# Second MLP: a plain tile of 256 tokens, four tiles of 512 by half-block products, and a plain last group

## The chip, the cores and the metric

The kernel runs on one core of a Trainium2 chip. The metric is the device time of one execution in microseconds (us); a lower one is better. Three executions of the kernel before took 1023.52, 1023.8 and 1024.66 us, median 1023.8.

## The reference

Three stages follow one another, all in fp32: causal attention with a bias for 4 sequences of 576 tokens and 8 heads of 64, a first MLP with softplus, a second MLP with a rational function. The change touches the second MLP:

```
x = _moe_ref(x=x, ...)                  # [2304, 512], the first MLP
h = x @ w_in                            # [2304, 512] @ [512, 2048]
P = a[0] + a[1]*h + a[2]*h*h + a[3]*h*h*h
Q = 1.0 + |b[0]|*|h| + |b[1]|*h*h
g = P / (Q + 1e-06)
return g @ w_out                        # [2304, 2048] @ [2048, 512]
```

## The kernel before

Every product of matrices is made of three products of fp32r parts: high by high, high by low, low by high. An operand therefore comes as a pair (`gh` and `gl` for g, `xh` and `xl` for x, `wh` and `wl` for a weight): ScalarE copies the high part, and GpSimd or VectorE subtracts it to get the low one.

The 2048 hidden units are 16 blocks of 128 (`ff`). For a tile of tokens and a block, the *first product* makes h in a bank of PSUM (tiles `h` and `at`, two banks each), an elementwise chain makes g, and the *second product* adds g times w_out to the output banks (`acc`, four of them, 128 tokens by 512 each).

The elementwise chain of a block is: ScalarE makes a = |h| (L1201, L1238), t (L1203, L1240) and w (L1202, L1239); GpSimd multiplies w by a (L1204, L1241); VectorE multiplies t by h and adds (L1205 and L1206, L1242 and L1243); then `quotient`: ScalarE Ln (L1219) and Exp (L1220), VectorE three passes (L1221 to L1223); then ScalarE copies the high part (L1395, L1254) and GpSimd makes the low one (L1397, L1255). The exponential is written back into the block's bank of PSUM, so that the bank comes free only after the last VectorE pass, L1223. In the first five blocks of the first tile (`H_ONLY`) it goes to SBUF instead.

The tiles of the second MLP are listed in `T2`: one *plain* tile of 384 tokens, three of 512, one plain tile of 384 (`TAIL`). In a plain tile the first product of a block is 12 products of all the tile's tokens (L1092 to L1094), the second is 3 for each 128 tokens (L1135 to L1137).

In a tile of 512 the blocks go in four groups (`q`), each of two by two half-blocks: a pair of hidden blocks i, and two halves j of the tokens. Four half-block pairs of first products are made of seven *slots* (`SLOTS`, L1340) in place of eight, from sums and differences of weights and of tokens; a slot is 12 products of 256 columns. The sums of slots are taken through a save in SBUF (ScalarE, L1361) and an addition (VectorE, L1366). `out_part` (L1269 to L1271) makes the second products. The operands of the slots are split by ScalarE and GpSimd (L1291, L1292), the weight parts `wa` come from DRAM by DMA.

While the first plain tile runs, VectorE, ScalarE and GpSimd still convert weights of the second MLP (L907 to L914), and the first three blocks are interleaved with the end of the first MLP.

The order of instructions on each engine is fixed by a planner (`plan`), which follows costs of operations up to the planned time `UNTIL`; what comes later stays in the order in which the events were written. Every engine takes its instructions in that order.

The last tile is copied out of PSUM by ScalarE and VectorE in turn (`evacuate`); the last 128 tokens go in two halves (L1156 to L1159).

Of the kernel before, what the change touches and what calls it, by code (L numbers as in the profile page):

```python
# [17 lines left out]
T2 = [(0, 384)] + [(384 + t * 512, 512) for t in range(3)] + [(1920, 384)]  # L18
TAIL = 4
# [4 lines left out]
KD = DM // 128  # L24
NF = DFF // 128
NEG = -8.0e9
LAST = (1, TAIL, 15)
# [41 lines left out]
UNTIL = 936.0  # L69
# [269 lines left out]
def moe_chain_kernel(ctx, tc, qk0, v0, qk, vv, s0, s, w1, w2, ab, out):  # L339
# [703 lines left out]
    def split_x_(ph, T, k):  # L1043
        n = TILES[ph][T][1]
        if n <= 256:
            t = t_xs([128, 2, 256])[:, :, 0:n]
            hi, lo = t[:, 0], t[:, 1]
        elif ph == 1 and k == 0:
            hi, lo = (y_t[T][:, KD + i] for i in range(2))
        elif (ph, T) == (1, TAIL):  # L1050
            hi, lo = (t_l("xl", [128, 512], F32R)[:, 0:n] for _ in range(2))
        else:
            hi, lo = t_xs([128, 512])[:, 0:n], t_xs([128, 512])[:, 0:n]
        if ph == 0:
            for b, s0, w, o in segments(T):
                nc.scalar.activation(hi[:, o:o + w], x_t[b][:, k, s0:s0 + w], AF.Copy)
                nc.vector.tensor_tensor(lo[:, o:o + w], x_t[b][:, k, s0:s0 + w], f(hi[:, o:o + w]), op=ALU.subtract)
        else:
            src = f(y_t[T][:, k])
# [6 lines left out]
    def load_y(T):  # L1066
        plain = T in (0, TAIL)
        y_t[T] = t_x("yt", [128, KD + 2 * plain, T2[T][1]], F32R if plain else F32)
        for a, o, n in pieces(*T2[T]):
            dst = y_t[T][:, 0:KD, o:o + n]  # L1070
            nc.sync.dma_start(out=f(dst) if plain else dst, in_=y_d[a])
# [5 lines left out]
    def stage_a_(u):  # L1077
# [6 lines left out]
        else:  # L1084
            wh, wl = w2_t[ff, 0] if T == 0 else (None, None)
        for k in range(KD):
            xh, xl = xs_t[ph, T, k]
            cs = slice(k * 128, (k + 1) * 128)
            if (ph, T) == (1, TAIL):
                w, cs = wa_t[T, ff // 4, f"a{ff % 2 + 1}{k // 2 + 1}"][:, ff // 2 % 2], slice(k % 2 * 128, k % 2 * 128 + 128)  # L1090
                wh, wl = w[:, 0], w[:, 1]
# [49 lines left out]
    def evacuate(ph, T, acc):  # L1141
# [10 lines left out]
        for m, a in enumerate(acc):  # L1152
            if (ph, T, m) == (1, TAIL, 2):
                ya, yb = (tmp_tile("PA", 3, (128, 256)) for _ in range(2))
                o = out[t0 + 256:t0 + 384, :]
                nc.scalar.activation(ya, a[:, 0:256], AF.Copy)  # L1156
                nc.vector.tensor_copy(yb, a[:, 256:512])
                nc.sync.dma_start(out=o[:, 0:256], in_=ya)
                nc.scalar.dma_start(out=o[:, 256:512], in_=yb)  # L1159
                return  # L1160
# [23 lines left out]
    def stage1_(u):  # L1184
# [11 lines left out]
        else:  # L1196
# [7 lines left out]
            (nc.vector if u == LAST else nc.gpsimd).tensor_tensor(w, w, a, op=ALU.mult)  # L1204
# [4 lines left out]
    def stage2(u):  # L1209
# [4 lines left out]
        r, o = (h_t[u],) * 2 if T or ff >= H_ONLY else (a, w)  # L1214
# [10 lines left out]
    class Block:  # L1225
        def __init__(self, T, q, i, j):
            self.T, self.q, self.i, self.j = T, q, i, j
            self.ends = q == 3 and i != j

    w_no = [0]  # L1230

    def act1(bl):
        h = bl.h
        a = tmp_tile("e", 2)
        t = tmp_tile("PA", 3, (128, 512))
        w = tmp_tile(*(("P4", 2), ("tc", 3), ("tmp", 1), ("tc", 3))[w_no[0] % 4], (128, 512))
        w_no[0] += 1
# [6 lines left out]
        bl.g = (t, w, a)  # L1244

    def act2(bl):
        t, w, a = bl.g
        quotient(a, t, w, bl.h, bl.h)
        bl.g = t

    def act3(bl):
        gh = tmp_tile("gh", 3, dt=F32R)
        gl = tmp_tile("gl", 3, dt=F32R)
        nc.scalar.activation(gh, bl.g, AF.Copy)  # L1254
        nc.gpsimd.tensor_tensor(gl, bl.g, f(gh), op=ALU.subtract)  # L1255
        bl.g = (gh, gl)
# [3 lines left out]
    def out_part(bl, p):  # L1260
        gh, gl = bl.g
# [17 lines left out]

    ops_t = {}  # L1280

    def operand_steps(T):
# [6 lines left out]
        def split(name, src):  # L1289
            hi, lo = ops_t[T, name] = new(name), new(name)  # L1290
# [3 lines left out]
        def minus(o, x, z):  # L1294
# [95 lines left out]
    def stage3_(u):  # L1390
# [5 lines left out]
        eng = nc.vector if in_bank(u) or u == LAST else nc.gpsimd  # L1396
# [4 lines left out]
    if True:  # L1401
# [195 lines left out]
        for T in range(1, TAIL):  # L1597
            at = 28 * (T - 1)
            for q in range(4):
                group(T, q, at + 7 * q, events)  # L1600
            events.append((at + 9.3, lambda T=T: load_y(T + 1)))
            for n in range(7):
                events.append(((at - 5.7 + n if T > 1 else 0.01 + 0.05 * n if n < 2 else 0.5 + 0.9 * n), lambda T=T, n=n: operand(T, n)))
        at = 28 * (TAIL - 1) + 1

        def tail_a(u):
            stage_a(u)
            used[0] += u[2] % 4 == 3 and 4
            load_wa(used[0] + WA_AHEAD)

        for k in range(KD):
            events.append((at - 4 + k, lambda k=k: split_x(1, TAIL, k)))
        for ff in range(NF):
            u = (1, TAIL, ff)
            for t, fn in ((0, tail_a), (0.1, stage1), (1.5, stage2), (2.9, stage3), (4.3, stage_b)):
                events.append((at + 1.4 * ff + t, lambda u=u, fn=fn: fn(u)))
# [65 lines left out]
```

## Time and profile before

| | |
|---|---|
| median of three executions | 1023.8 us |
| profiled execution, its own time | 1024.89 us |
| span of the profiled execution | 1023.1 us |
| granted TensorE clock, mean | 1.000 |
| busy: TensorE | 998.2 us (98%) |
| busy: ScalarE | 803.2 us (79%) |
| busy: VectorE | 791.1 us (77%) |
| busy: GpSimd | 466.4 us (46%) |

The span reaches from the first to the last instruction; the execution's own time is 1.8 us longer. The first plain tile of the second MLP runs from about 616 to 687 us, the three half-block tiles follow to 940, the last plain tile to 1019. In the tables, PE is TensorE's products, PEld its weight loads, DVE VectorE, ACT ScalarE, POOL GpSimd; SPq and ACTq are the queues from which transfers are issued. Busy times of products overlap, so what one product costs is read from start to start.

### The profile page before, as it was taken

Reading aid. Unit: us, or ns where it says so; the run is one execution under the profiler, and the core shown is the slowest. Engines: PE = TensorE matmul, PEld = TensorE weight load, DVE = VectorE, ACT = ScalarE, POOL = GpSimd, SP = SyncE. Lnnn points to the kernel's source line nnn. Section 1 sums busy time; section 2 is a strip of 40 time slices with the busy share of each in tenths; the row PEclk is TensorE's granted clock in tenths of the full one; section 3 lists DMA queues with packets and bytes.
Section 4 is the critical chain, followed back from the end, with each engine's and each line's share of the span. In section 5 each row is a group of like instructions: output and inputs, shape, how many; then the busy total and the mean of one; then the engine's idle time right before and its main releaser. Section 6 shows DMA issues by size and latency. Waiting matters only on the chain. (4 is left out here: it accounts for less than half of the span.)

```text
span 1023.1 us, 18253 instructions
## 1 busy us (share of the span) xinstructions
PE 998.2 (98%) x5924; PEld 903.1 (88%) x5924; DVE 791.1 (77%) x1783; ACT 803.2 (79%) x1652; POOL 466.4 (46%) x464
## 2 busy tenths in 40 slices
PE   6999999999999999999999999999999999999998
PEld 5889999898999888988999999888888998889897
DVE  5888987878897888786677549888788778777765
ACT  5898878887887777777767778888779878788775
POOL 2756665311220121121445666765567457555542
PEclk9999999999999999999999999999999999999999
DMA  9877566565554653435999998528456656555300
GB/s 249 292 253 240 189 220 215 167 206 163 154 189 145 194 166 121 121 101 173 370 342 336 300 351 285 184 83 273 168 167 208 206 168 191 206 169 160 124 1 31
DMA packets 101071, 201.63 MB, mean 197 GB/s; under 512 B 11249, under 2 KB 30513, under 8 KB 100977
## 3 DMA queue, kind: packets, MB, share of 16 engines
q1 hardware_dynamic: 98432, 196.31, 58.6%
q10 hardware_dynamic: 2544, 4.16, 1.6%
q8 instruction: 47, 0.77, 0.3%
q14 instruction: 48, 0.39, 0.1%
HBM read 161.16 MB, written 35.19 MB: 192 GB/s over the span
## 5 line engine op out<-in xcount | busy, mean ns | idle before, releaser
L614 POOL TENSOR_SCALAR PA<-PA,stat 128x384 f32<-128x384 f32 (+3 forms) x112 | 70.8, 638 | 173.1 <-DVE stat L613 65.7
L1092 PE MATMUL h<-xs,w1h 128*128 128x448 f32 (+1 forms) x360 | 122.8, 342 | 1.6 <-DVE e L1194 1.5
L1093 PE MATMUL h<-xs,w1h 128*128 128x448 f32 (+1 forms) x360 | 122.7, 341 | 0.0
L1094 PE MATMUL h<-xs,w1l 128*128 128x448 f32 (+1 forms) x360 | 122.1, 340 | 0.0
L1129 PE MATMUL acc<-gl,w1h 128*128 128x448 f32 (+1 forms) x352 | 118.9, 339 | 1.2 <-POOL gl L1397 1.2
L1130 PE MATMUL acc<-gh,w1l 128*128 128x448 f32 (+1 forms) x352 | 118.5, 340 | 0.8 <-DMA w1l<-l_d 0.7
L1128 PE MATMUL acc<-gh,w1h 128*128 128x448 f32 (+1 forms) x352 | 118.6, 340 | 0.0
L1255 POOL TENSOR_TENSOR gl<-PA,gh 128x512 fp32r<-128x512 f32 x48 | 63.2, 1319 | 69.8 <-issue 55.9
L611 ACT ACTIVATE PA<-PA,stat 128x384 f32<-128x384 f32 (+3 forms) x112 | 64.0, 572 | 17.4 <-DVE stat L594 16.2
L1269 PE MATMUL acc<-w2b,gh 128*128 128x512 f32 x192 | 75.9, 395 | 0.0
L1270 PE MATMUL acc<-w2b,gh 128*128 128x512 f32 x192 | 75.8, 395 | 0.0
L1271 PE MATMUL acc<-w2b,gl 128*128 128x512 f32 x192 | 73.7, 395 | 0.0
L1092 PEld LDWEIGHTS h<-xs,w1h 128*128 128x128 f32 x360 | 67.8, 189 | 5.8 <-DVE e L1194 2.4
L1093 PEld LDWEIGHTS h<-xs,w1h 128*128 128x128 f32 x360 | 67.8, 188 | 3.4
L1094 PEld LDWEIGHTS h<-xs,w1l 128*128 128x128 f32 x360 | 67.8, 189 | 3.1
L1129 PEld LDWEIGHTS acc<-gl,w1h 128*128 128x128 f32 x352 | 66.1, 188 | 4.5 <-POOL gl L1397 1.4
L1130 PEld LDWEIGHTS acc<-gh,w1l 128*128 128x128 f32 x352 | 66.0, 189 | 4.4 <-DMA w1l<-l_d 0.9
L1128 PEld LDWEIGHTS acc<-gh,w1h 128*128 128x128 f32 x352 | 66.1, 189 | 3.0
L1190 ACT ACTIVATE e<-h 128x448 f32<-128x448 f32 (+1 forms) x90 | 43.3, 482 | 30.3 <-PE h L1094 28.6
L1397 POOL TENSOR_TENSOR gl<-e,gh 128x256 fp32r<-128x256 f32 (+1 forms) x48 | 47.4, 989 | 31.1 <-ACT gh L1395 25.6
L594 DVE CUSTOM_DVE_ANT_0 PA<-at,mask 128x384 f32<-128x384 f32 (+3 forms) x100 | 50.5, 518 | 5.7 <-PE at L622 4.2
L621 PE MATMUL at<-ht 128*128 128x512 f32 (+3 forms) x156 | 53.5, 347 | 1.1 <-DVE stat L602 0.8
(353 smaller groups left out, 3187.7 us busy)
## 6 DMA issues: line engine op xcount, KB each, us to landing
wa<-wa_d SPq DMA_DIRECT2D x100, 512.0 KB
w1l<-l_d SPq DMA_DIRECT2D x138, 256.0 KB
raw<-in_w_dram SPq DMA_DIRECT2D x48, 512.0 KB
raw<-in_qk_dram SPq DMA_DIRECT2D x24, 384.0 KB
l_d<-w1l SPq DMA_DIRECT2D x32, 256.0 KB
raw64x<-in_w_dram SPq DMA_DIRECT2D x16, 512.0 KB
wa_d<-pt SPq DMA_DIRECT2D x16, 512.0 KB
raw<-in_qk_dram SPq DMA_DIRECT2D x8, 576.0 KB
```

The source lines that it names most:

```text
L611: nc.scalar.activation(pt[:, 0:n], pt[:, 0:n], AF.Exp, bias=mn, scale=-1.0, accum_out=stat[:, i, 1:2])
L614: nc.gpsimd.tensor_scalar(pt[:, 0:n], pt[:, 0:n], stat[:, i, 2:3], 1.0, op0=ALU.mult, op1=ALU.mult)
L1092: nc.tensor.matmul(h, wh[:, cs], xh, start=(k == 0), stop=False)
L1093: nc.tensor.matmul(h, wh[:, cs], xl, start=False, stop=False)
L1094: nc.tensor.matmul(h, wl[:, cs], xh, start=False, stop=(k == KD - 1))
L1128: nc.tensor.matmul(o, wh[:, cs], gh, start=first and not both, stop=False)
L1129: nc.tensor.matmul(o, wh[:, cs], gl, start=False, stop=False)
L1130: nc.tensor.matmul(o, wl[:, cs], gh, start=False, stop=last and (not both or m % 2 == 1))
L1255: nc.gpsimd.tensor_tensor(gl, bl.g, f(gh), op=ALU.subtract)
L1269: nc.tensor.matmul(acc[m], gh[:, cs], wh, start=first, stop=False)
L1270: nc.tensor.matmul(acc[m], gh[:, cs], wl, start=False, stop=False)
L1271: nc.tensor.matmul(acc[m], gl[:, cs], wh, start=False, stop=last)
```

## The change

The first plain tile has 256 tokens instead of 384, there are four half-block tiles of 512 in place of three, and the plain tile at the end is gone. In the last group (q = 3) of the last tile the first products of the blocks 12 to 15 are plain: `last_a` makes a block in 24 products of 256 columns, `last_b` adds its second product. The last block goes through the elementwise chain in two halves of 256 columns, with VectorE in GpSimd's place. The outputs of the last group leave from tiles of the pool PA, which has three buffers. The operand b12, which seven slots do not need, is split for this group alone. `store_a` stores for the blocks below 12 only what is loaded again, and `UNTIL` goes from 936 to 966. The bounds of the first MLP's output pieces follow from the tiles, so that these shift too.

```diff
-T2 = [(0, 384)] + [(384 + t * 512, 512) for t in range(3)] + [(1920, 384)]
-TAIL = 4
+T2 = [(0, 256)] + [(256 + t * 512, 512) for t in range(4)]
-UNTIL = 936.0
+UNTIL = 966.0
...
     def store_a(ff, ts):
+        b0 = ff % 2 if ff < FS else 0
         for h, t in enumerate(ts):
-            nc.sync.dma_start(out=row_a(ff)[:, :, h], in_=f(t).rearrange("p (b c) -> p b c", b=2))
+            nc.sync.dma_start(out=row_a(ff)[:, b0:, h], in_=f(t).rearrange("p (b c) -> p b c", b=2)[:, b0:])
...
-        nc.gpsimd.tensor_tensor(w, w, a, op=ALU.mult)
+        (nc.vector if bl.final else nc.gpsimd).tensor_tensor(w, w, a, op=ALU.mult)
...
-        nc.gpsimd.tensor_tensor(gl, bl.g, f(gh), op=ALU.subtract)
+        (nc.vector if bl.final else nc.gpsimd).tensor_tensor(gl, g, f(gh), op=ALU.subtract)
...
+    def last_a(ff):
+        T, i, p = len(T2) - 1, ff % 2, ff // 2 % 2
+        bl = Block(T, 3, i, 0)
+        bl.ff, bl.final = ff, ff == NF - 1
+        bl.h = bank(hsel(1, T, ff))
+        for j in range(2):
+            o = bl.h[:, j * 256:j * 256 + 256]
+            for k in range(KD):
+                w, (xh, xl) = wa_t[T, 3, f"a{i + 1}{k // 2 + 1}"], ops_t[T, f"b{k // 2 + 1}{j + 1}"]
+                cs = slice(k % 2 * 128, k % 2 * 128 + 128)
+                wh, wl = w[:, p, 0, cs], w[:, p, 1, cs]
+                for n, (x, z) in enumerate(((wh, xh), (wh, xl), (wl, xh))):
+                    nc.tensor.matmul(o, x, z[:, k % 2], start=j == k == n == 0, stop=(k, n) == (KD - 1, 2),
+                                     skip_group_check=True)
+        return bl
+
+    def last_b(bl, j):
+        T, (gh, gl) = bl.T, bl.o
+        wh, wl = w2_t[bl.ff, 1]
+        acc = acc2[T, j]
+        for m in range(2):
+            cs = slice(j * 256 + m * 128, j * 256 + m * 128 + 128)
+            nc.tensor.matmul(acc[m], gh[:, cs], wh, start=False, stop=False)
+            nc.tensor.matmul(acc[m], gh[:, cs], wl, start=False, stop=False)
+            nc.tensor.matmul(acc[m], gl[:, cs], wh, start=False, stop=bl.final)
+            if bl.final:
+                t0 = T2[T][0] + j * 256 + m * 128
+                cut = ((0, 256), (256, 512)) if j == m == 1 else ((0, 512),)
+                for n, (a, b) in enumerate(cut):
+                    y = tmp_tile("PA", 3, (128, 512))[:, a:b]
+                    if n == (m + 1) % 2:
+                        nc.scalar.activation(y, acc[m][:, a:b], AF.Copy)
+                    else:
+                        nc.vector.tensor_copy(y, acc[m][:, a:b])
+                    for b0, s0, w, o in tokens(t0, 128):
+                        (nc.scalar if n else nc.sync).dma_start(out=out[b0 * S + s0:b0 * S + s0 + w, a:b], in_=y[o:o + w])
...
+        at += 21
+        last_t = {}
+        for n in range(4):
+            t = at + 2 * n
...
+            halves = [ALL] if n < 3 else [slice(0, 256), slice(256, 512)]
+            for d, fn in ((0.1, act1), (2.1, act2), (4.1, act3)) if n < 3 else ((0.1, act1), (1.1, act2), (2.1, act3)):
+                for k, c in enumerate(halves):
+                    events.append((t + d + 0.2 * k, lambda ff=FS + n, fn=fn, c=c: fn(last_t[ff], c)))
+            for j in range(2):
+                events.append((t + 6.2 + 0.1 * j, lambda ff=FS + n, j=j: last_b(last_t[ff], j)))
```

In the changed kernel the numbers of lines are others: the chain of a half-block's elementwise work is L1225 to L1230 (before L1238 to L1243), the quotient L1201 to L1205 (before L1219 to L1223), the high and low parts L1242 and L1243 (before L1254 and L1255). In the following rows a number behind a name tells one tile from another, and the brackets say whom an instruction waits for.

ScalarE at the end of the last half-block tile, before; `at_11401` is the bank that the last slot completes, `h_11643` the first block of the plain tile behind it:

```order
L1219 ACTIVATE e_11541<-tc_11543,prm_123 128x512 [waits Pool_49]
L1220 ACTIVATE h_11539<-e_11541 128x512 [waits DVE_49,Activation_49]
L1238 ACTIVATE e_11623<-at_11401 128x512 [waits PE_49,Activation_49]
L1219 ACTIVATE e_11585<-tmp_11587,prm_123 128x512 [waits Pool_49]
L1239 ACTIVATE tc_11625<-e_11623,prm_123 128x512 [waits Activation_49]
L1220 ACTIVATE h_11491<-e_11585 128x512 [waits DVE_49,Activation_49]
L1254 ACTIVATE gh_11671<-PA_11542 128x512 [waits DVE_49]
L1240 ACTIVATE PA_11624<-at_11401,prm_123 128x512
L1219 ACTIVATE e_11623<-tc_11625,prm_123 128x512 [waits Pool_49]
L1254 ACTIVATE gh_11707<-PA_11586 128x512 [waits DVE_49]
L1201 ACTIVATE e_11656<-h_11643 128x384 [waits PE_49,Activation_49]
L1220 ACTIVATE at_11401<-e_11623 128x512 [waits DVE_49,Activation_49]
```

ScalarE at the same place of the last half-block group (q = 2) after the change; `at_12080` is the bank that its last slot completes, `h_12274` the plain block 12, which TensorE fills 60 products later:

```order
L1242 ACTIVATE gh_12334<-PA_12204 128x512 [waits DVE_49]
L1242 ACTIVATE gh_12382<-PA_12242 128x512 [waits DVE_49,PE_49]
L1225 ACTIVATE e_12301<-h_12274 128x512 [waits PE_49,Activation_49]
L1227 ACTIVATE PA_12299<-h_12274,prm_123 128x512
L1226 ACTIVATE tc_12300<-e_12301,prm_123 128x512 [waits Activation_49]
L1225 ACTIVATE e_12310<-at_12080 128x512
L1227 ACTIVATE PA_12308<-at_12080,prm_123 128x512 [waits Pool_49]
L1226 ACTIVATE P4_12309<-e_12310,prm_123 128x512 [waits Activation_49]
L1201 ACTIVATE e_12301<-tc_12300,prm_123 128x512 [waits Pool_49]
L1201 ACTIVATE e_12310<-P4_12309,prm_123 128x512 [waits Pool_49]
L1202 ACTIVATE h_12274<-e_12301 128x512 [waits DVE_49,Activation_49]
L1202 ACTIVATE at_12080<-e_12310 128x512 [waits DVE_49,Activation_49]
```

The Abs of the last slot's bank stood ahead of the two copies of high parts and of the next block's Abs; now it stands behind both.

TensorE at the last block's first product, before (`at_12284`, block 15 of the plain tile, in between the second products of block 12):

```order
L1137 MATMUL acc_11785<-w2b_8050,gl_12241 128x512
L1135 MATMUL acc_11786<-w2b_8050,gh_12240 128x512
L1092 MATMUL at_12284<-yt_10999,wa_11782 128x384 [waits DVE_49]
L1136 MATMUL acc_11786<-w2b_8050,gh_12240 128x512
L1093 MATMUL at_12284<-yt_10999,wa_11782 128x384
L1137 MATMUL acc_11786<-w2b_8050,gl_12241 128x512
L1094 MATMUL at_12284<-yt_10999,wa_11782 128x384
```

TensorE there after the change (`at_12463`, block 15, goes into the bank of `at_12080`; `gh_12392` and `gl_12393` are the parts of the block made from `at_12080`):

```order
L1258 MATMUL acc_11926<-w2b_7994,gl_12383 128x512
L1279 MATMUL at_12463<-xl_11363,wa_12023 128x256 [waits DVE_49,PE_49]
L1279 MATMUL at_12463<-xl_11364,wa_12023 128x256
L1279 MATMUL at_12463<-xl_11363,wa_12023 128x256 x2
L1279 MATMUL at_12463<-xl_11364,wa_12023 128x256
L1279 MATMUL at_12463<-xl_11363,wa_12023 128x256
L1256 MATMUL acc_11837<-w2b_7950,gh_12392 128x512 [waits Activation_49]
L1257 MATMUL acc_11837<-w2b_7950,gh_12392 128x512
L1258 MATMUL acc_11837<-w2b_7950,gl_12393 128x512 [waits Pool_49]
```

Block 15 and the second product behind it now both depend on the block made from `at_12080`.

ScalarE at the very end, before:

```order
L1220 ACTIVATE at_12284<-e_12311 128x384 [waits DVE_49,Activation_49]
L1395 ACTIVATE gh_12351<-PA_12312 128x384 [waits DVE_49,PE_49]
L1164 ACTIVATE yb_12364<-acc_11784 128x512 [waits DMAHW2_49,DMAHW4_49,DMAHW1_49,PE_49]
L1156 ACTIVATE PA_12369<-acc_11786 128x256 [waits PE_49,Pool_49]
L1159 DMA out_0_dram<-PA_12370 128x256 [waits DMAHW0_49,DVE_49]
```

and after the change:

```order
L1202 ACTIVATE at_12463<-e_12499 128x256 [waits DVE_49,Activation_49]
L1242 ACTIVATE gh_12544<-PA_12497 128x256 [waits PE_49]
L1242 ACTIVATE gh_12544<-PA_12497 128x256 [waits DVE_49]
L1298 ACTIVATE PA_12583<-acc_11838 128x512 [waits PE_49,Pool_49]
L1298 ACTIVATE PA_12595<-acc_11926 128x256 [waits DMAHW6_49,DVE_49,PE_49]
L1302 DMA out_0_dram<-PA_12598 128x256 [waits DMAHW2_49,DVE_49]
```

The copy of the first half of the last 128 tokens now waits for a transfer (DMAHW6), too: its buffer is that of the first of the five tiles.

## Rows read from the trace of the kernel before

**Rows 1.** The page: span, and each engine's busy time, share and instructions.
```profile
span 1023.1 us, 18253 instructions
...
PE 998.2 (98%) x5924; PEld 903.1 (88%) x5924; DVE 791.1 (77%) x1783; ACT 803.2 (79%) x1652; POOL 466.4 (46%) x464
```

**Rows 2.** Stretches: length, busy time of each engine, clock, DMA share, GB/s.
```profile
core 0: us, PE busy (x) PEld busy (x) DVE busy (x) ACT busy (x) POOL busy (x), PEclk, DMA share, GB/s
616.00:650.00 34.00, 33.16 (x169) 29.86 (x168) 31.85 (x47) 26.99 (x54) 22.03 (x18) 1.00 0.76 255
...
703.00:770.00 67.00, 65.28 (x405) 57.86 (x404) 53.66 (x78) 54.01 (x91) 38.78 (x30) 1.00 0.59 200
855.00:940.00 85.00, 85.00 (x532) 76.29 (x531) 65.86 (x100) 70.38 (x119) 46.19 (x37) 1.00 0.58 188
940.00:1019.00 79.00, 78.49 (x384) 68.97 (x382) 54.58 (x97) 59.41 (x111) 36.29 (x35) 1.00 0.16 48
1019.00:1023.10 4.10, 0.34 (x2) 0.00 (x0) 0.79 (x2) 0.38 (x1) 0.00 (x0) 0.91 0.54 192
```

**Rows 3.** Waits of TensorE, 560 to 1023: total us, times, longest.
```profile
PE at L1340 <- ACT pt L1361: 1.6, 2, 1.3
```

**Rows 4.** Timeline of TensorE, in two places: start, us, engine, line, operation.
```profile
658.77 0.34 PE L1094 MATMUL at<-xs,w2a 128*128 128x384 f32 x1
...
659.99 0.39 PE L1135 MATMUL acc<-w2b,gh 128*128 128x512 f32 x1
...
936.84 0.40 PE L1269 MATMUL acc<-w2b,gh 128*128 128x512 f32 x1
...
938.24 1.59 PE L1340 MATMUL at<-xs,wa 128*128 128x256 f32 x12
939.67 0.40 PE L1269 MATMUL acc<-w2b,gh 128*128 128x512 f32 x1
```

**Rows 5.** Timeline of ScalarE and VectorE, 941 to 950.
```profile
941.02 0.60 ACT L1238 ACTIVATE e<-at 128x512 f32<-128x512 f32 x1
941.51 0.71 ACT L1219 ACTIVATE e<-tmp,prm 128x512 f32<-128x512 f32 x1
...
949.82 0.74 DVE L1223 SCALAR_TENSOR_TENSOR PA<-PA,prm,at 128x512 f32<-128x512 f32 x1
```

**Rows 6.** Groups by line, 855 to 940: busy us, mean ns, idle before.
```profile
L1238 ACT ACTIVATE e<-h 128x512 f32<-128x512 f32 x13 | 7.7, 595 | 2.4 <-DVE h L1366 1.8
L1240 ACT ACTIVATE PA<-h,prm 128x512 f32<-128x512 f32 x13 | 10.1, 774 | 0.0
L1239 ACT ACTIVATE tc<-e,prm 128x512 f32<-128x512 f32 x8 | 6.5, 811 | 0.0
L1219 ACT ACTIVATE e<-tc,prm 128x512 f32<-128x512 f32 x9 | 6.5, 721 | 0.2 <-POOL tc L1241 0.2
L1220 ACT ACTIVATE h<-e 128x512 f32<-128x512 f32 x12 | 7.2, 602 | 0.8 <-DVE PA L1243 0.6
...
L1222 DVE SCALAR_TENSOR_TENSOR h<-tc,h 128x512 f32<-128x512 f32 x4 | 2.8, 696 | 0.1
...
L1241 POOL TENSOR_TENSOR tc<-tc,e 128x512 f32<-128x512 f32 x9 | 11.7, 1300 | 5.5 <-ACT tc L1239 5.5
```

**Rows 7.** Timeline at the end: last product, last copy.
```profile
1018.94 0.40 PE L1137 MATMUL acc<-w2b,gl 128*128 128x512 f32 x1
...
1019.92 0.42 DVE L1157 COPY PA<-acc 128x256 f32<-128x256 f32 x1 [0.56 <-ACT PA L1156]
```

**Rows 8.** VectorE's groups by line, 616 to 687.
```profile
L1222 DVE SCALAR_TENSOR_TENSOR P<-P,e 128x384 f32<-128x384 f32 x2 | 2.8, 1390 | 0.0
...
L1222 DVE SCALAR_TENSOR_TENSOR h<-P,h 128x384 f32<-128x384 f32 x2 | 1.1, 556 | 0.0
```

More of the change, by code (lines that the diff above doesn't have):

```diff
@@ L26 @@
 NEG = -8.0e9
-LAST = (1, TAIL, 15)
 N_H = 2
@@ L1047, in split_x_ @@
             hi, lo = t[:, 0], t[:, 1]
[L1048 to L1051, printed above, removed]
         else:
@@ L1066, in load_y @@
     def load_y(T):
-        plain = T in (0, TAIL)
-        y_t[T] = t_x("yt", [128, KD + 2 * plain, T2[T][1]], F32R if plain else F32)
+        y_t[T] = t_x("yt", [128, KD, T2[T][1]], F32)
         for a, o, n in pieces(*T2[T]):
-            dst = y_t[T][:, 0:KD, o:o + n]
-            nc.sync.dma_start(out=f(dst) if plain else dst, in_=y_d[a])
+            nc.sync.dma_start(out=y_t[T][:, :, o:o + n], in_=y_d[a])
     def stage_a(u):
@@ L1084, in stage_a_ @@
         else:
-            wh, wl = w2_t[ff, 0] if T == 0 else (None, None)
+            wh, wl = w2_t[ff, 0]
         for k in range(KD):
@@ L1152, in evacuate @@
         for m, a in enumerate(acc):
[L1153 to L1160, printed above, removed]
             i = a[:, 0:n]
@@ L1203, in stage1_ @@
             nc.scalar.activation(t, h, AF.Identity, scale=nega[:, 3:4], bias=nega[:, 2:3])
-            (nc.vector if u == LAST else nc.gpsimd).tensor_tensor(w, w, a, op=ALU.mult)
+            nc.gpsimd.tensor_tensor(w, w, a, op=ALU.mult)
             nc.vector.tensor_tensor(t, t, h, op=ALU.mult)
@@ L1213, in stage2 @@
         a, t, w = e_t[u]
-        r, o = (h_t[u],) * 2 if T or ff >= H_ONLY else (a, w)
+        r, o = (h_t[u],) * 2 if ff >= H_ONLY else (a, w)
         quotient(a, t, w, r, o)
@@ L1228, in __init__, with act1 @@
             self.ends = q == 3 and i != j
+            self.final = False
+            self.g = self.o = None
     w_no = [0]
[L1232 to L1237, printed above, removed]
+    ALL = slice(0, 512)
+    def act1(bl, c=ALL):
+        if bl.g is None:
+            bl.g = (tmp_tile("PA", 3, (128, 512)),
+                    tmp_tile(*(("P4", 2), ("tc", 3), ("tmp", 1), ("tc", 3))[w_no[0] % 4], (128, 512)), tmp_tile("e", 2))
+            w_no[0] += 1
+        h = bl.h[:, c]
+        t, w, a = (x[:, c] for x in bl.g)
         nc.scalar.activation(a, h, AF.Abs)
@@ L1289, in split @@
         def split(name, src):
-            hi, lo = ops_t[T, name] = new(name), new(name)
+            if name == "b12":
+                both = t_x("b12", [128, 2, 2, 256], F32R)
+                hi, lo = ops_t[T, name] = both[:, 0], both[:, 1]
+            else:
+                hi, lo = ops_t[T, name] = new(name), new(name)
             nc.scalar.activation(hi, src, AF.Copy)
@@ L1395, in stage3_ @@
         nc.scalar.activation(gh, g, AF.Copy)
-        eng = nc.vector if in_bank(u) or u == LAST else nc.gpsimd
+        eng = nc.vector if in_bank(u) else nc.gpsimd
         eng.tensor_tensor(gl, g, f(gh), op=ALU.subtract)
@@ L1595, in operand, with start @@
             steps[T][n]()
-        for T in range(1, TAIL):
+        for T in range(1, len(T2)):
             at = 28 * (T - 1)
-            for q in range(4):
+            for q in range(4 if T + 1 < len(T2) else 3):
                 group(T, q, at + 7 * q, events)
-            events.append((at + 9.3, lambda T=T: load_y(T + 1)))
+            if T + 1 < len(T2):
+                events.append((at + 9.3, lambda T=T: load_y(T + 1)))
             for n in range(7):
                 events.append(((at - 5.7 + n if T > 1 else 0.01 + 0.05 * n if n < 2 else 0.5 + 0.9 * n), lambda T=T, n=n: operand(T, n)))
[L1604 to L1616, printed above, removed]
+        at += 21
+        last_t = {}
+        for n in range(4):
+            t = at + 2 * n
+            def start(ff=FS + n):
+                last_t[ff] = last_a(ff)
+            events.append((t, start))
+            halves = [ALL] if n < 3 else [slice(0, 256), slice(256, 512)]
[4 more added lines that the diff above has]
+                events.append((t + 6.2 + 0.1 * j, lambda ff=FS + n, j=j: last_b(last_t[ff], j)))
         region[0] = 2
```

33 lines of the change are left out of this document (15 added, 18 removed).

## The prediction

> **What bounds the kernel now.** I read the page's engine totals first: TensorE is busy 998.2 of 1023.1 us [rows 1]. The stretch table comes next, since the change lies in the second MLP alone. There the reader is to see that TensorE is idle 0.84 us of the first 34 us, 1.72 us where the first half-block tile begins (703 to 770), nothing in the third such tile (855 to 940), and 0.51 us from 940 to 1019 [rows 2]. So this stage is TensorE work almost from end to end: an edit gains what it takes from TensorE's queue, and every wait that it makes is paid in full. The second thing in the same table is what stands close behind: VectorE is busy 31.85 of the first 34 us (94%), whereas ScalarE has 70.38 of 85 us and VectorE 65.86 of 85 us in the half-block tile. The waits of TensorE in this stage are few, and the longest stands ahead of the half-block products, on ScalarE's save L1361 (1.6 us in two) [rows 3].
>
> **TensorE's work.** A 384-column product starts 0.174 us after the one before it (seven from 658.77 to 659.99), a 512-column one 0.233 us (six from 936.84 to 938.24), a 256-column one 0.119 us (twelve from 938.24 to 939.67) [rows 4]. The plain tile of 384 tokens has 16 blocks of 12 products of 384 columns and 9 of 512: 192 x 0.174 + 144 x 0.233 = 67.0 us, and there are two of them. A half-block tile has 28 slots of 12 products of 256 columns and 192 products of 512: 336 x 0.119 + 192 x 0.233 = 84.7 us, in agreement with the 85.0 us of the table. Three of these and two plain ones make 388.1 us. After the change the plain tile of 256 tokens has 192 x 0.119 + 96 x 0.233 = 45.2 us, four half-block tiles 338.8 us, and the last group, plain, has 4 blocks of 24 products where seven slots of 12 stood: 12 more, +1.4 us. That is 385.4 us. Between the rounded 2.7 and a sum that takes the half-block tile at its measured 85.0 us I take **-2.6 us**.
>
> What a product costs beside its columns matters here, since the change has 9,216 columns less but 156 products more: 0.119 us for 256 columns and 0.233 for 512 put 0.005 us on every product, and 0.174 for 384 is in line. The Trainium skill (TensorE: Matmul & The Clock Gate, section "Wait — 56ns, not 53.3ns?") gives columns over 2.4 GHz and some 2.5 ns per product; by it the work would fall by 3.84 - 0.39 = 3.45 us, an estimate. These rows, all at full granted clock, lie 5 to 10% above its price, so I stay with them.
>
> **The last group.** This is the dearest new wait, and it follows from the order in which ScalarE takes its work. Take as zero the end of the last product of the slot that completes "at" (939.67 in the third half-block tile of before [rows 4]). In before, ScalarE takes the Abs of that bank 1.35 us later, at 941.02, and VectorE's last pass over it starts at 949.82, ends at 950.56 and sets the bank free [rows 5], 10.9 us after the zero. In the changed kernel the Abs of a bank that TensorE fills only afterwards (block 12) stands ahead of it in ScalarE's queue. TensorE's queue until that block: 12 products of 512 columns (2.8 us), 24 of 256 for block 13 and 24 for block 12 (2.86 each), so block 12 is complete at 8.5. From there, with a ScalarE operation starting some 0.1 us before the one ahead of it has ended (0.49 between 941.02 and 941.51 at a duration of 0.60 [rows 5]) and the durations of [rows 6]: Abs, t and w of block 12 from 8.6, Abs, t and w of the waiting bank from 10.5 to 12.45; GpSimd's two products of 1.30 us end at 11.9 and 13.75; the two logarithms at 13.05 and 14.5, the two exponentials at 15.0 and 15.5; then six VectorE passes in turn at 0.65 from start to start, the last ending at 19.05. TensorE wants this bank for block 15 at 8.5 + 1.4 + 2.86 + 1.4 + 2.8 = 17.0. It waits 2.1 us.
>
> It then runs 6 products (to 19.8) and stands before the second product of the same waiting block, whose high part ScalarE makes at 19.4 to 20.0 and whose low part GpSimd makes behind the w*a products of blocks 13 and 14, that is 17.4 + 3 x 1.30 = 21.3. Less the two products that need the high part alone, this is 1.2 us more. Queued behind are 90-odd products of TensorE with nothing else to do, so 3.3 us is paid. The 0.51 us of today's end part goes; **+2.8 us**. Bounds: -0.5 if the bank is free by 17.0 after all; +6 if the last block's chain is late as well (2.1 + 1.2 + a third wait of the size of a GpSimd product and a VectorE pass, some 2.7 us).
>
> **The last stores.** Today 0.79 MB leave in the 4.1 us after 1019 (192 GB/s) [rows 2], and the last chain is product at 1018.94, VectorE copy at 1019.92 that waited 0.56 us for ScalarE's read of the same bank [rows 7], store, end at 1023.1. After the change the last 512 tokens have 1 MB of output, in five tiles out of a pool of three, so the fourth copy waits for the store of the first and the fifth for that of the second. The missing 0.26 MB at 192 GB/s is 1.35 us at most; nothing at least, if the earlier stores leave while TensorE still works. I take **+0.6 us**, nearer the middle because the first two stores are issued some 1.5 us ahead of the last product.
>
> **The first tile.** Its five first blocks keep the quotient in SBUF and share VectorE with weight conversions, which do not shrink. VectorE's passes over a block fall from about 0.55 us to about 0.42 (the 256-column copy of [rows 7]): 25 passes, -3.3 us. TensorE's part of a block falls from 12 x 0.174 + 9 x 0.233 = 4.2 us to 12 x 0.119 + 6 x 0.233 = 2.83, so it asks for the fifth block some 4.5 x (4.2 - 2.83) = 6.2 us earlier. With the 2.15 us that VectorE has free in 34 today [rows 2], 0.75 us is lacking; a part of the 0.84 us of idle time today is the same shortage. I take **+0.6 us**. At the least, today's 0.84 goes. At the most: a VectorE pass over SBUF alone took 1390 ns against 556 with a PSUM operand [rows 8], and if all ten such passes of the five blocks went at 1.39 x 256/384 = 0.93 instead of 0.37 us, they would cost 5.6 us, of which today's four slow ones are paid already: +4 us.
>
> The Trainium skill has a rule for these rows (SBUF — State Buffer, section "🔬 SBUF: two separate sides"): a VectorE operation with two SBUF inputs and a GpSimd operation that reads SBUF lock each other out for a whole instruction. The 1390 against 556 ns agree, and by it the narrower passes would still wait for GpSimd's 512-wide conversions; that is the upper end above, told here as a rival.
>
> The start of the first half-block tile, with its 1.6 us on L1361, I leave as it is: 0, up to +2.1, since the blocks whose second products cover it have 6 instead of 9 products (3 x 3 x 0.233). The half-block tiles, their joints, the halved store of a weight part and the small moves of the earlier stages I cost at 0, within 1 us either way: the third tile shows no idle time to gain or to lose [rows 2].
>
> **Sum.** -2.6 + 2.8 + 0.6 + 0.6 = +1.4 us. The profiled execution took 1024.89 us (span 1023.1), 1.09 over the median of 1023.8; 1024.89 + 1.4 - 1.09 = **1025.2 us**, within 0.2% of before. The bound of 0.2% (2.05 us: 1021.75 to 1025.85) is about what a measurement of this kernel can tell.
>
> **Rivals.** *The saving stands.* The bank is free when TensorE comes for it, since that rests on a chain of some sixteen steps of which each could be a tenth of a microsecond shorter, or TensorE comes later because it has waited elsewhere. Then -2.6 - 0.5 + 0.6 + 0.6 = -1.9, or -2.5 without the first tile's term: 1021.3 to 1021.9, and 1020.5 if the stores hide too. For it: TensorE had only 0.51 us of idle time in the end part of before, with as long chains. Against it: the order puts a bank that is ready at 0 behind one that is ready at 8.5. Chance 0.31.
>
> *The first tile becomes VectorE's.* The passes over SBUF go at the slow price: place, the first five blocks; point from which it decides, VectorE's load above TensorE's 2.83 us per block. It is 94% loaded today. +4 instead of +0.6: 1028.6, slower than before. Against it: three of the five blocks are interleaved with the first MLP's last products, which gives VectorE time. Chance 0.20.
>
> *The start of the half-block tiles.* Less second-product work covers L1361: +2.1 on top of the forecast, 1027.3. For it: that wait is the longest today. Chance 0.12.
>
> *The change does no more than shift its work* is the forecast: what TensorE saves is waited away in the last group. Chance 0.37.
>
> So faster 0.31, same 0.37, slower 0.32. For 8 in 10 the range goes from 1020.4 (saving with hidden stores) to 1028.8 (VectorE bound); the forecast's own range is 1023.5 to 1026.5.
>
> **What would show it.** In the changed kernel's profile: TensorE's work from the first block of the plain tile to the end, without idle time, some 385.5 us; a wait of about 2 us ahead of L1279 for block 15, released by VectorE L1205 over "at", and one of about 1 us ahead of the second product, on GpSimd L1243; the last copies L1298 and L1300 released by a DMA (lines of the changed kernel); idle time of TensorE in the first five blocks of 1 to 2 us. The forecast is wrong if TensorE comes to block 15 and finds the bank free, or if it is idle for more than 3 us in the plain tile.

## The result and the profile after

The changed kernel is slower. Its median over four executions is 1031.86 us (1028.39 to 1035.49), that of the kernel before 1024.23 us (1023.52 to 1025.87); the ratio is 1.0073, 95% interval 1.0055 to 1.0091. Two more sets of pairs gave 1.0046 (1.0031 to 1.0061) and 1.0055 (1.0040 to 1.0070). The prediction was 1025.2 us, no change, with a range up to 1028.8 us: it was wrong, and the whole range lies too low.

The profiled execution took 1028.39 us (span 1026.6) and is the shortest of the four. It has a granted clock of 1.000 throughout; the other three have 0.994 to 0.998. So two questions follow: where the 3.5 us of the profile come from, and what the others lost beside them.

The stretches of the changed kernel: plain tile, one half-block tile, last half-block tile with the last group, end. The columns are those of [rows 2].

```profile
616.00:665.00 49.00, 48.23 (x300) 43.13 (x299) 43.77 (x85) 43.04 (x104) 34.68 (x38) 1.00 0.72 241
...
751.00:837.00 86.00, 85.23 (x529) 75.93 (x529) 67.96 (x99) 69.78 (x118) 51.39 (x40) 1.00 0.63 204
...
922.00:1021.00 99.00, 95.19 (x568) 83.04 (x567) 71.29 (x112) 73.77 (x127) 47.19 (x37) 1.00 0.26 81
1021.00:1026.60 5.60, 0.69 (x3) 0.21 (x2) 1.12 (x2) 0.38 (x1) 0.00 (x0) 1.00 0.52 187
```

TensorE is idle 0.77 us in the plain tile, about as long as before (0.84 in the first 34 us), and 3.81 us in the last stretch, where it was idle 0.51 us from 940 to 1019 [rows 2]. The half-block tile of before from 855 to 940 had no idle time; the one from 751 to 837 here has 0.77. TensorE's waits in this stage, as in [rows 3]:

```profile
PE at L1279 <- DVE PA L1205: 2.1, 1, 2.1
PE h L1368 <- PE at L1368: 1.5, 2, 0.8
PE at L1368 <- ACT pt L1389: 1.4, 2, 0.9
PE acc L1258 <- POOL gl L1243: 0.8, 2, 0.7
```

The first, and 0.7 of the 0.8 us of the last, are the two waits of the last group. Here are TensorE, ScalarE and VectorE there (timeline), the rows that answer to [rows 5]; the first one is the slot that completes the bank:

```profile
981.98 1.58 PE L1368 MATMUL at<-xs,wa 128*128 128x256 f32 x12
...
992.77 0.60 ACT L1225 ACTIVATE e<-h 128x512 f32<-128x512 f32 x1 [1.90 <-PE h L1279]
...
994.63 0.59 ACT L1225 ACTIVATE e<-at 128x512 f32<-128x512 f32 x1
...
1000.72 0.40 PE L1258 MATMUL acc<-w2b,gl 128*128 128x512 f32 x1
1002.38 0.74 DVE L1205 SCALAR_TENSOR_TENSOR PA<-PA,prm,at 128x512 f32<-128x512 f32 x1
1003.27 0.94 PE L1279 MATMUL at<-xl,wa 128*128 128x256 f32 x6 [2.15 <-DVE PA L1205]
1004.63 0.40 PE L1257 MATMUL acc<-w2b,gh 128*128 128x512 f32 x1
1005.70 0.50 PE L1258 MATMUL acc<-w2b,gl 128*128 128x512 f32 x1 [0.67 <-POOL gl L1243]
```

ScalarE stands idle for 1.90 us until TensorE has filled block 12, and only behind that block's first three operations, at 994.63, takes the Abs of the bank that had been ready since about 983.5, for 11 us. VectorE's last pass frees that bank at 1003.12; TensorE had come to it at about 1000.95. From start to start TensorE loses 2.31 us ahead of block 15 and 0.24 and 0.83 us around the next second product, 3.4 us in all.

The end of the changed kernel (timeline), which answers to [rows 7]:

```profile
1021.29 0.40 PE L1291 MATMUL acc<-w2b,gl 128*128 128x512 f32 x1
1022.82 0.38 ACT L1298 ACTIVATE PA<-acc 128x256 f32<-128x256 f32 x1 [1.88 <-DMA out_dram<-PA]
1023.46 0.42 DVE L1300 COPY PA<-acc 128x256 f32<-128x256 f32 x1 [1.50 <-DMA out_dram<-PA]
1023.92 0.38 ACTq L1302 DMA_DIRECT2D out_dram<-PA  x1
```

Both last copies wait for the store of an earlier tile. From the last product's start to the end it is 5.3 us, where it was 4.16 [rows 7].

### The profile page after: what moved, and what is told of

Read it like the earlier page. It is cut to its first block, busy times and chain, and to the rows that moved or that the text cites. A ratio compares the mean times of both kernels' runs of the same rounds, so it can differ in the third digit from the quotient of the medians.

```text
span 1026.6 us, 18649 instructions
## 1 busy us (share of the span) xinstructions
PE 997.5 (97%) x6080; PEld 900.0 (88%) x6080; DVE 795.5 (77%) x1801; ACT 807.7 (79%) x1670; POOL 477.6 (47%) x472
## 3 DMA queue, kind: packets, MB, share of 16 engines
q10 hardware_dynamic: 2544, 4.16, 1.6%
## 4 chain that ended last, share of the span: by engine, by line
PE 78%; DVE 8%; ACT 6%; POOL 4%; issue 3%; DMA 2%; SPq 0%; POOLq 0%; DVEq 0%; ACTq 0%
PE at L1368 7%; PE h L1082 5%; PE at L760 5%; PE h L1368 5%; PE h L1083 5%; PE h L1084 5%; PE acc L1120 5%; PE acc L1118 5%; PE acc L1119 5%; PE acc L1258 4%; PE acc L1257 4%; PE acc L1256 4%; PE at L619 3%; PE at L620 2%; PE at L695 1%
## 5 line engine op out<-in xcount | busy, mean ns | idle before, releaser
L1243 POOL TENSOR_TENSOR gl<-PA,gh 128x512 fp32r<-128x512 f32 x63 | 83.5, 1326 | 84.3 <-issue 62.7
L1256 PE MATMUL acc<-w2b,gh 128*128 128x512 f32 x240 | 95.1, 396 | 0.1
L1257 PE MATMUL acc<-w2b,gh 128*128 128x512 f32 x240 | 94.8, 395 | 0.0
L1258 PE MATMUL acc<-w2b,gl 128*128 128x512 f32 x240 | 92.6, 397 | 0.9 <-POOL gl L1243 0.8
L1242 ACT ACTIVATE gh<-PA 128x512 fp32r<-128x512 f32 (+1 forms) x65 | 40.4, 623 | 35.4 <-DVE PA L1205 35.2
```

Source lines behind the costliest of these rows:

```text
L1243: (nc.vector if bl.final else nc.gpsimd).tensor_tensor(gl, g, f(gh), op=ALU.subtract)
L1256: nc.tensor.matmul(acc[m], gh[:, cs], wh, start=first, stop=False)
L1257: nc.tensor.matmul(acc[m], gh[:, cs], wl, start=False, stop=False)
L1258: nc.tensor.matmul(acc[m], gl[:, cs], wh, start=False, stop=last)
```

## The experiments

Eleven runs were made in four sets of pairs, of nine kernels: the changed one and minus_pool_late stand twice. Each set has its own executions of the kernel before, and the ratios are to these.

**again** and **again_2**: no edit.

> The changed kernel once more, unaltered. Its first runs went from 1028.4 to 1035.5 us, at mean granted clocks from 1.000 down to 0.994. Theory A (the granted clock falls in some runs behind the waits of TensorE in the last group, between 1000 and 1006 us): a run of more than 1030 us shows a stretch of lower clock that begins after 1000 us. Theory B (it falls elsewhere, for example in the plain tile of 256 tokens or at the joints of the half-block tiles): the stretch begins between 616 and 930 us. Both expect a time between 1028 and 1036 us.

> The changed kernel unaltered, for a second set of pairs. The theory by now: in each execution TensorE waits 2.15 us ahead of block 15 and 0.7 us for GpSimd, and in most executions the granted clock then falls to half for a stretch of some 3.4 us that begins at 1004 to 1006 us, which costs 1.7 us. It expects 1028 to 1031 us and mean clocks of 0.997 or 0.998, against 0.999 to 1.000 of kernels without the wait. A rival: the clock falls more than once in some executions (the first set had 1035.5 us at a clock of 0.994), then a profile with less than 0.997 shows two or more stretches.

The two sets gave 1029.55 us (1028.70 to 1030.16) at mean clocks of 0.997 and 0.998, and 1030.14 us (1029.22 to 1030.64) at the same. The profile of the first has the fall. Stretches of it, the last but two column being the granted clock:

```profile
1000.00:1004.00 4.00, 1.85 (x10) 1.26 (x9) 4.00 (x7) 3.92 (x7) 1.88 (x2) 1.00 0.00 0
...
1005.00:1006.00 1.00, 0.40 (x2) 0.00 (x0) 0.00 (x0) 1.00 (x3) 1.00 (x2) 0.76 0.00 0
1006.00:1007.00 1.00, 0.92 (x2) 0.82 (x3) 0.66 (x2) 0.93 (x2) 1.00 (x2) 0.50 0.00 0
1007.00:1008.00 1.00, 1.00 (x4) 0.71 (x4) 1.00 (x3) 0.00 (x0) 0.27 (x1) 0.50 0.00 0
1008.00:1009.00 1.00, 1.00 (x7) 1.00 (x6) 1.00 (x3) 0.00 (x0) 0.00 (x0) 0.53 0.00 0
1009.00:1010.00 1.00, 1.00 (x11) 1.00 (x10) 0.57 (x1) 0.00 (x0) 0.00 (x0) 1.00 0.00 0
```

and TensorE in the same profile (timeline):

```profile
1006.68 0.63 PE L1256 MATMUL acc<-w2b,gh 128*128 128x512 f32 x1
1007.10 0.63 PE L1257 MATMUL acc<-w2b,gh 128*128 128x512 f32 x1
1007.53 0.63 PE L1258 MATMUL acc<-w2b,gl 128*128 128x512 f32 x1
```

The reader is to see TensorE busy 1.85 of 4 us, then 0.40 of 1 us, and then, at 1005.5, the clock at 0.50, that is 1.2 in place of 2.4 GHz, for about 3.4 us (0.24/0.5 + 1 + 1 + 0.47/0.5). In it 512-column products start 0.43 us apart instead of 0.233. If TensorE worked all through such a stretch, it would cost some 1.6 us (0.20 of every 0.43); but it spends 0.6 us of this one waiting. From the start of block 15 to the start of the last product the profile without a fall has 18.02 us, again 19.32 and again_2 19.51, so that the fall costs 1.3 and 1.5 us. (The whole times of these two executions differ by 1.5 us, 1029.92 against 1028.39, but that is another sum: the plain tile of again already starts 1.1 us later.) Theory A holds for the two profiles; that of again_2 has the same stretch at 1006.0, and no other in its second MLP. The clocks of the other six executions, 0.997 and 0.998, fit, though a mean clock counts the end as well, where it costs nothing: in again the clock is at 0.50 once more from 1026.0 on, 3 us behind the last product.

The first set stays open in part. Its three other executions took 1030.70, 1033.01 and 1035.49 us at 0.996, 0.998 and 0.994, and none of them has a profile. A mean clock of 0.998 (0.9975 or more) is worth 2.6 us at most, not the 4.6 us by which the execution of 1033.01 us lies above the profiled one. Nor does any profile show two falls in one execution, the rival of again_2.

**abs_first**: the last group's events begin 0.2 later, so that the order of two blocks in the text of the program turns round.

```diff
-        at += 21
+        at += 21.2
```

> The last group's events begin at +21.2 in place of +21, so that the elementwise chain of the last half-block's bank is written ahead of block 12's and takes its tiles first; nothing else is altered. ScalarE then takes the Abs of that bank when its slot ends. Theory A: the wait of TensorE ahead of block 15 (2.15 us) and the one on GpSimd's low part (0.7 us) go, the profile is about 3 us shorter than that of the changed kernel (1025.4 us at full clock), and with the waits the falls of the clock go too, so that all runs lie within 2 us. Theory B: the profile gains the same 3 us, but runs at a lower clock stay, with a spread of several us.

It gave 1025.65 us (1023.96 to 1026.78, ten executions), ratio 1.0005 (0.9996 to 1.0015) to the kernel before, clocks of 0.999 and 1.000. ScalarE's Abs of the bank and TensorE at block 15 (timeline):

```profile
988.66 0.58 ACT L1225 ACTIVATE e<-at 128x512 f32<-128x512 f32 x1
...
1004.09 0.39 PE L1258 MATMUL acc<-w2b,gl 128*128 128x512 f32 x1
1004.32 1.59 PE L1279 MATMUL at<-xl,wa 128*128 128x256 f32 x12
```

Block 15 starts 0.23 us after the product ahead of it: no wait is left. From the first product of the plain tile to the last product it is 402.90 us in place of 406.46. So a number in a table of events cost 3.5 us of the profile, and in the same set of pairs, with the falls of the clock, 3.9 us of the median (1029.55 to 1025.65). Block 12's chain was written at +21.1, the last half-block's at +21.2; that the order acts through the pool of tiles, where whoever is written first takes its tiles first, is read from the program and was not tested by itself.

**stores_tc**: the halves of the last 128 tokens in tiles of another pool.

```diff
-                    y = tmp_tile("PA", 3, (128, 512))[:, a:b]
+                    y = tmp_tile("tc" if len(cut) > 1 else "PA", 3, (128, 512))[:, a:b]
```

> The two halves of the last 128 tokens are copied into tiles of another pool (tc), so that neither copy waits for the store of an earlier tile. Of the 1.15 us by which the end from last product to last instruction grew (4.16 to 5.3 us), theory 1 (the copies' waits of 1.88 and 1.50 us for a transfer) expects 1.0 us back; theory 2 (the extra 256 KB of output and the bandwidth of the stores) expects at most 0.3 us back. The waits in the last group stay, and the spread with them.

The end (timeline):

```profile
1022.09 0.40 PE L1291 MATMUL acc<-w2b,gl 128*128 128x512 f32 x1
1022.52 0.38 ACT L1298 ACTIVATE tc<-acc 128x256 f32<-128x256 f32 x1 [0.79 <-PE acc L1291]
1022.94 0.42 DVE L1300 COPY tc<-acc 128x256 f32<-128x256 f32 x1 [0.19 <-ACT tc L1298]
...
1023.39 0.38 ACTq L1302 DMA_DIRECT2D out_dram<-tc  x1
```

From the last product's start to the end (1026.50) it is 4.4 us: 0.9 of the 1.15 us came back, so theory 1 holds. The median, 1029.37 us (1028.29 to 1030.98), does not tell this from the changed kernel's, since the waits of the last group are still there (clocks 0.997 and 0.998).

**abs_and_stores**: both.

> Both edits together. If they are independent, the profile is 4 us shorter than that of the changed kernel: about 1024.3 us, no different from the kernel before. If the stores bound the end whenever TensorE ends earlier, it is only 3 us shorter.

1024.79 us (1023.98 to 1025.17), ratio 0.9997 (0.9987 to 1.0006). The two add up as expected, and with them the change is worth nothing, neither gain nor loss, though TensorE has 2.8 us less to do.

**before_late_abs**: the kernel before, with the order of the same two chains turned round.

```diff
-        at = 28 * (TAIL - 1) + 1
+        at = 28 * (TAIL - 1)
```

> The kernel before, with the events of its last plain tile begun at +0 in place of +1. Nothing else is altered, but the chain of block 0 is now written ahead of the chain of the last half-block's bank, so that ScalarE takes the Abs of that bank after the Abs of block 0, as in the changed kernel. Theory A (the inverted order costs a wait only as far as TensorE has too little work in front of that bank): TensorE comes to the bank some 15.5 us after the slot's end, the bank is free at 15 to 16, so the wait is under 1 us, the clock does not fall, and the time is that of the kernel before within 0.1%. Theory B (the inversion itself is the cost): about +3 us, as in the changed kernel.

1024.55 us (1023.55 to 1026.61), ratio 1.0006 (0.9997 to 1.0015). The bank is free when TensorE comes; the wait that is left is this one (timeline):

```profile
962.97 0.50 PE L1137 MATMUL acc<-w2b,gl 128*128 128x512 f32 x1 [0.90 <-POOL gl L1397]
```

Theory A holds: the inverted order costs only what TensorE's work in front of the bank doesn't cover.

**seven_last**: the last group by seven slots; the events of `last_a` and `last_b` are gone.

```diff
-            for q in range(4 if T + 1 < len(T2) else 3):
+            for q in range(4):
```

> The changed kernel with the last group by seven slots instead of four plain blocks: 12 products fewer (-1.4 us of TensorE's work). If the plain last group was no use, the profile is 1.4 us shorter than that of the changed kernel, or more. If the last chain binds (after the last slot TensorE has 48 second products, 11.2 us, of which half need blocks whose chain takes 10.9 us and more), TensorE waits 3 to 8 us in the last 15 us, the clock falls there, and the time is 1030 us or more.

1030.38 us (1029.52 to 1030.60), ratio 1.0059 (1.0043 to 1.0076). TensorE (timeline) and the stretch behind its wait:

```profile
1008.16 0.39 PE L1258 MATMUL acc<-w2b,gl 128*128 128x512 f32 x1
1013.05 0.50 PE L1256 MATMUL acc<-w2b,gh 128*128 128x512 f32 x1 [4.50 <-ACT gh L1242]
```

```profile
1013.70:1017.10 3.40, 3.11 (x8) 2.15 (x7) 2.87 (x5) 1.03 (x2) 1.80 (x2) 0.50 0.00 0
```

Without the plain last group the last chain stands bare for 4.5 us, and the clock falls here too. Against the changed kernel as it stands this is no difference (1030.14 us in the same set): the plain group's own waits eat its gain. Against abs_first, where its order is right, it is one: ratios of 1.0005 and 1.0059, some 5 us, though from two sets.

**minus_pool**: on top of abs_and_stores, the operands' subtractions on GpSimd.

```diff
-            nc.vector.tensor_tensor(o, x, z, op=ALU.subtract)
+            nc.gpsimd.tensor_tensor(o, x, z, op=ALU.subtract)
```

> The kernel with both edits (abs_and_stores), and the five subtractions that make a tile's operands moved from VectorE to GpSimd. At the three joints of half-block tiles TensorE waits 0.9, 0.9 and 0.2 to 0.7 us for a bank of h, whose chain on VectorE is pushed back by these subtractions (0.69 us each) in two of the three. If VectorE is what binds there, 1 to 2 us come back: 1022.8 to 1023.8 us. If GpSimd's longer instructions (1.30 us) push its low parts back instead, the joints cost the same or more: 1024.8 us or later.

1028.19 us (1025.88 to 1028.62), ratio 1.0031 (1.0018 to 1.0044): slower. But the joints are closed. Two joints in abs_and_stores and the same in minus_pool (stretches):

```profile
751.00:765.00 14.00, 13.23 (x81) 11.66 (x80) 11.28 (x18) 13.19 (x24) 10.81 (x9) 1.00 0.68 223
837.00:850.00 13.00, 12.29 (x76) 10.90 (x76) 10.32 (x16) 12.69 (x23) 9.80 (x8) 1.00 0.57 183
```

```profile
668.00:700.00 32.00, 26.85 (x176) 23.62 (x174) 17.78 (x31) 23.15 (x43) 25.86 (x24) 1.00 0.63 208
751.00:765.00 14.00, 14.00 (x97) 12.93 (x96) 9.74 (x15) 13.19 (x23) 13.81 (x12) 1.00 0.60 202
836.00:850.00 14.00, 14.00 (x95) 12.86 (x94) 9.57 (x15) 12.95 (x23) 13.39 (x12) 1.00 0.55 174
```

The 0.77 and 0.71 us of idle time are gone; at the start of the first half-block tile TensorE now stands idle for 5.15 of 32 us. There GpSimd, busy for 25.86 of them, has the operands to make in one go, at 1.3 us a subtraction.

**minus_pool_late** and its repetition **minus_pool_late_2**: the same, but for the first half-block tile on VectorE. **before_minus_pool**: the kernel before with this edit alone.

```diff
-            nc.vector.tensor_tensor(o, x, z, op=ALU.subtract)
+            (nc.vector if T == 1 else nc.gpsimd).tensor_tensor(o, x, z, op=ALU.subtract)
```

> The kernel with both edits (abs_and_stores), with the operand subtractions on GpSimd for the second to fourth half-block tile only, and on VectorE for the first. In minus_pool the waits at the three joints went (some 2.1 us in all) and the start of the first tile lost 5 us. If the two are independent, this kernel is 2 us shorter than abs_and_stores: from the first product of the plain tile to the last product 400 us in place of 402.0, a time of 1022.3 to 1022.9 us, faster than the kernel before. If the joint only hands its wait on to the next group, it stays at 1024 to 1025 us.

> The fastest kernel so far once more. Its executions fell into two groups, 1020.9 to 1022.1 us at a mean clock of 0.999 and 1023.4 to 1024.8 us at 0.997 to 0.998; the one with a profile was of the first group. The theory (a long single wait of TensorE lets the granted clock fall in many executions) expects the stretch of half clock, if the profile has one, right behind the wait of 2.4 us at the start of the first half-block tile (689 to 692 us), some 3.4 us long. If it lies elsewhere, another cause is at work. The median is expected at 1022 to 1024 us, below the kernel before in both.

> The kernel before with the same edit alone: subtractions of the second and third half-block tile on GpSimd. Its joint at 767 to 776 us has 1.3 us of waits, the other none. If VectorE binds the joint here too, 1.0 to 1.3 us come back (1023.2 to 1023.6 us where the kernel before has 1024.5); if the wait there is another one, nothing changes.

minus_pool_late is faster than the kernel before: 1023.35 us (1020.94 to 1024.82), ratio 0.9986 (0.9976 to 0.9995), and in the repetition 1023.26 us, 0.9982 (0.9972 to 0.9991). From the first product of the plain tile to the last product it takes 400.1 us in both profiles, as expected. The time is above the 1022.3 to 1022.9 us that were expected with it: the executions are 2.0 to 2.55 us longer than their spans, those of abs_and_stores 1.8, and twelve of the twenty-two have the lower clocks spoken of below; no run says why. The edit alone does nothing: before_minus_pool has 1023.97 us, ratio 0.9996 (0.9987 to 1.0005). The waits at its joint went, but its plain tile, which the planner ordered anew, has a wait on ScalarE that was 0.4 us before (waits):

```profile
PE acc L1135 <- ACT gh L1395: 1.5, 1, 1.5
```

The planner gave minus_pool_late another order, too, on all engines and from about 670 us on, so that what closes the joints is the edit together with this order. What is left in minus_pool_late is the start of the first half-block tile (timeline, then stretch):

```profile
688.67 0.88 PE L1368 MATMUL at<-xs,wa 128*128 128x256 f32 x6
691.96 0.72 PE L1368 MATMUL h<-xl,wa 128*128 128x256 f32 x4 [2.41 <-issue]
```

```profile
688.70:692.00 3.30, 0.89 (x9) 0.71 (x7) 3.30 (x7) 2.91 (x6) 0.91 (x1) 1.00 1.07 374
```

TensorE waits 2.41 us while the DMA engines are busy throughout (share 1.07, 374 GB/s); that it waits for a weight part is likely, but no run took the transfer away. The question of the second expectation, where the clock falls in this kernel's longer executions (0.997 and 0.998, 1023.3 to 1025.0 us), stays open: both profiles are of executions without a fall inside.

## Why the prediction was wrong, step by step

**TensorE's work, -2.6 us: right.** From the first product of the plain tile to the last product it was 403.10 us, and is 406.46; in this time TensorE's starts lie 5.8 and 11.9 us later than the distances of [rows 4] make them. So the work fell by 11.9 - 5.8 - 3.36 = 2.7 us; this sum takes the distances as given and cannot test them. What does is the changed kernel's own trace: where it has no wait, 256 columns start 0.119 us apart (1523 products) and 512 columns 0.233 (843). With each trace's own distances the work is 388.1 and 385.3 us, 2.8 less. The price of a product from the rows held. The estimate by the rule of the Trainium skill that the prediction weighed (TensorE: Matmul & The Clock Gate, section "Wait — 56ns, not 53.3ns?") was 3.45 us; the traces do not agree with it.

**The last group, +2.8 us: the mechanism and its length right, its price wrong. This is the step that failed.** The wait came to 2.31 us where 2.1 was worked out, the one on GpSimd and its forerunner to 1.07 where 1.2 was: 3.4 against 3.3 us. (By the prediction's own times the second part is 1.0, not 1.2: 0.2 us until the high part is there at 20.0, and 0.8 from the two products' end at 20.5 to 21.3.) The prediction paid the wait at its length, "so 3.3 us is paid", and put what TensorE's clock does behind it at nothing. again and again_2 show it: half clock for 3.4 us, another 1.3 and 1.5 us. The twenty executions with a wait of more than 2 us in their last group (the changed kernel, again, again_2, stores_tc, seven_last) have mean clocks of 0.994 to 0.998 but for one, the profiled one; those of abs_first and abs_and_stores, twenty too, 0.999 or 1.000. The edit that takes away the wait takes away the fall, too. Without this price the pairs of again and again_2 would give 3.4 and 4.2 us in place of 4.7 and 5.7; the range ended 5.0 us above the 1023.8 that it started from. For the 7.6 us of the first set the price is not enough, and the rest of them stays open.

**The last stores, +0.6 us: right in kind, half in size.** 1.15 us, near the upper bound of 1.35; 0.9 of it is the wait for a buffer (stores_tc).

**The joints of the half-block tiles, 0 within 1 us: wrong, and about as dear as the clock.** The sum of TensorE's waits at the joints went from 1.3 to 3.0 us in the profile, and to 2.2 us in again. The prediction took the third tile of before, whose stretch has no idle time, as typical, but the idle time in the same trace stood at the joint from the first tile to the second, and the change has one joint more. One wait at that joint of before, and one in the changed kernel with the VectorE pass that ends just ahead of it (timeline):

```profile
767.90 1.70 PE L1340 MATMUL at<-xs,wa 128*128 128x256 f32 x12 [0.42 <-DVE h L1366]
```

```profile
837.39 0.69 DVE L1203 SCALAR_TENSOR_TENSOR tc<-tc,h 128x512 f32<-128x512 f32 x1 [0.90 <-ACT h L1202]
...
838.84 0.75 DVE L1205 SCALAR_TENSOR_TENSOR PA<-PA,prm,h 128x512 f32<-128x512 f32 x1
839.69 1.07 PE L1368 MATMUL h<-xl,wa 128*128 128x256 f32 x7 [0.71 <-PE at L1368]
```

The last VectorE pass over a bank of h ends at 839.59, and TensorE goes on at 839.69. minus_pool and minus_pool_late close the joints by taking the making of the next tile's operands off VectorE, in a new order. That VectorE is short there is likely but not shown: it had itself waited 0.90 us for ScalarE's exponential ahead of these passes.

**The start of the half-block tiles, 0, up to +2.1 us:** +0.4 us (waits of 1.9 us in place of 1.45), inside its bounds.

**The plain tile, +0.6 us, up to +4: wrong, it cost nothing.** Its waits sum to 1.4 us, as before. The rival of VectorE as the bound falls with it, though the slow passes were there: in the changed kernel (groups of VectorE's, 612 to 665)

```profile
L1203 DVE SCALAR_TENSOR_TENSOR P<-P,e 128x256 f32<-128x256 f32 x2 | 1.6, 808 | 0.6 <-ACT e L1202 0.6
...
L1204 DVE SCALAR_TENSOR_TENSOR h<-P,h 128x256 f32<-128x256 f32 x2 | 0.8, 420 | 0.0
```

808 against 420 ns is 1.9 times, where [rows 8] had 2.5 (1390 against 556). VectorE had room for it: it was busy for 43.77 of the 49 us from 616 to 665. That this is so because three of the five blocks are interleaved with the first MLP, as the rival's counter-argument had it, no run shows.

Summed up for the profile: -2.7 (work) + 3.1 (waits of the last tile: 3.9, 0.53 of it ahead of block 12, less 0.83 before) + 1.15 (end) + 1.7 (joints) + 0.4 (start of the half-block tiles) = +3.65 us; some 0.9 more are gaps under 0.12 us each. The span grew by 3.5, the part ahead of the plain tile being 1.0 us shorter in this execution. In again, with the fall in it, that part is as long as before: its span is 5.0 us longer, 3.9 from the first product of the plain tile to the last and 1.0 behind it, which is about what the pairs gave (4.7 and 5.7).

## What to carry to other kernels

Where engines take their work in the order in which it was written, two chains in the wrong order make an engine wait for the later one first; look at who is queued ahead of a bank that is ready, and at how much work the engine behind it has until it wants the bank: the same inversion cost 3.4 us here and nothing that the pairs could tell in before_late_abs. A wait of the engine that bounds is priced at its length and at what its clock may lose behind it, here 0.6 to 1.5 us. And a stretch without idle time between two joints says nothing about the joints.

## What had not been expected of the hardware

In the four profiles with a fall (again, again_2, stores_tc, seven_last) TensorE's clock was granted at half, 1.2 in place of 2.4 GHz, for 3.4 us each time. What TensorE did ahead of it differs. In again and again_2 it had stood idle for 2.15 us and then for 0.68 us, in seven_last for 4.5 us. In stores_tc 2.15 us alone came ahead: the clock fell at 1003.8, 0.3 us after TensorE had gone on and before the second wait (stretches).

```profile
1000.00:1004.00 4.00, 1.85 (x10) 1.30 (x9) 3.96 (x8) 3.92 (x7) 2.05 (x2) 0.98 0.00 0
1004.00:1005.00 1.00, 1.00 (x5) 0.99 (x5) 0.69 (x1) 1.00 (x3) 0.94 (x2) 0.50 0.00 0
```

The fall cost 0.6 us there (18.63 us from block 15 to the last product in place of 18.02), since part of it lay under the second wait, which shrank from 0.67 to 0.20 us. Nor does a wait of this length always bring a fall: the profiled execution of the changed kernel has both waits at a clock of 1.000, and the two profiles of minus_pool_late have none behind their 2.41 us. In minus_pool TensorE lost more, 5.15 of 32 us at the start of the first half-block tile, in several waits of at most 1.6 us, and its five executions have a mean clock of 1.000.
